# Stores of weight and matrix forms on GpSimd's queue, and earlier places for block 3's rows and block 2's x

## The chip, the core and the metric

The kernel runs on one core of a Trainium2 chip. A core has TensorE (PE; the trace shows its weight loads apart, as PEld), VectorE (DVE), ScalarE (ACT), GpSimd (POOL) and SyncE (SP), each with a queue of instructions that it works off in order, and 16 DMA engines that move data between HBM and the on-chip memory. The metric is the device time of one execution in microseconds, less is better; times of runs are medians.

## The reference

x has 2048 rows of 640. Its layer norm goes through a Fourier mixing (two products with 640x640 matrices, then two with 2048x2048 matrices) and beside it through a dense layer of 1536 with gelu. All is float32.

```python
xn = layernorm(x)                                   # (2048, 640), eps 1e-5
a = einsum("bsd,ed->bse", xn, dft_hid_re)           # wr
b = einsum("bsd,ed->bse", xn, dft_hid_im)           # wi
y = einsum("ts,bse->bte", dft_seq_re, a) - einsum("ts,bse->bte", dft_seq_im, b)
h = gelu_tanh(einsum("bsd,df->bsf", xn, w1) + b1)
out = x + y + einsum("bsf,fd->bsd", h, w2) + b2
```

## The kernel before

Every product is made of three matmuls of 128x128 by 128x512: an operand is split into a high part (an ACT pass, `AF.Copy` to float32r) and a low part (a DVE subtraction), and high x high, high x low and low x high are added up (`product`, `split`, `form_of`). The kernel therefore needs ACT and DVE for every operand that PE takes. Everything is written out by hand in program order: an instruction that waits holds up all behind it on its engine. DMAs are issued by SP, by ACT and, after the change, by GpSimd.

The rows of x are worked on in four blocks of 512. The dense layer comes first. **Block 0 and block 1** run through a loop over `g`, 24 steps: step `g` makes `hidden(g + 2)` (15 matmuls), `gelu(g + 2)`, and `output(g)` (15 matmuls). Beside the 12 steps of block 1, `second_block(i)` prepares what follows, and `prep_w(k)` turns and splits one part of the 640x640 matrices (wr, wi) into seven "forms" w0 to w6, which `put_w` stores to HBM (`wits`) from a staging buffer `wst`. A `prep_w` step is one of three: k = 0 stores two forms, k = 1 two, k = 2 three; six steps lie in block 1's loop, nine come later.

**Blocks 2 and 3** go through the dense layer together, in a scheme that saves products: their turned rows are combined into sums (a11, a12, a22, s1 to s4, oa, ob), likewise pairs of w1 columns (`sums_w1`, `split_w1`, loaded by `load_rq`). For six pairs q, `head(q)`, `mid(q)` and `finish(q)` make the products on eight PSUM banks, some of which are copied one to another by ACT (`copy_bank`, L803). The first of these pairs begins while block 1 ends: `head(0)` stands between `output(22)` and `output(23)`, and `mid(0)` needs bank 3, in which block 1's first output column was added up. `outs(1, ...)` empties those banks: ACT adds the bias (L344), DVE transposes into one of two small buffers (L347), GpSimd adds to `xo` (L349), and SP stores it (`ys`, L876).

The rows of block 3 come by this way: `ln_apply` (L201) normalises them, 16 DMAs (L203) store them to `xs`, `load_z(3)` reads them back in another order (L234), `turn_z2` and `turn_z1` transpose them (L732, L738).

After the pairs, block 2's outputs and then block 3's are added up by `second(2, ...)` and `second(3, ...)`, 24 steps `n`, each beside `beside_second(n)`. There `formed(k)`, four times, builds the forms of a piece of the mixing matrix, and stores them to HBM as `forms_ab` and `forms_c`; the latter from the one staging buffer `xcst`. `load_xr` loads the rows for the builds, `load_xo(2)` the x that `outs(2, ...)` adds to, into a tile that also holds raw w2 (`wz`), which `late_w2` splits. At last come the mixing's long products, a loop without forms of w to store.

Of the kernel before, what the change touches and what calls it, by code (L numbers as in the profile page):

```python
# [10 lines left out]
F32 = mybir.dt.float32  # L11
# [15 lines left out]
def kernel(  # L27
# [57 lines left out]
    def pool(name, side="left", stack=ctx):  # L85
        return stack.enter_context(tc.tile_pool(name=name, bufs=1, side=side, reuse_waits="tile"))
# [288 lines left out]
        )  # L375

    WEARLY = 2
    stores = []

    def put_away():  # L380
        for f in stores:
            f()
        stores.clear()

    def put_w(w, j, main, odd=None, negative=False):

        n = GWIDE[w] * P
        if A["w"]:
            t = A["w"].tile([P, 2, 3 * P], F32R, tag="wst", bufs=2, name=f"wst{w}_{j}")
        else:  # L390
            A["nst"] = A.get("nst", -1) + 1
            t = A["wst"][:, A["nst"] % 5 * 6 * P :][:, : 6 * P].rearrange("p (a b) -> p a b", a=2)
        split(t[:, 0, : 2 * P], t[:, 1, : 2 * P], main)
        if odd is not None and not negative:
            split(t[:, 0, 2 * P :], t[:, 1, 2 * P :], odd)
        elif odd is not None:
            h, l = t[:, 0, 2 * P :], t[:, 1, 2 * P :]
            nc.scalar.activation(h, odd, AF.Copy, scale=-1.0)
            nc.vector.scalar_tensor_tensor(l, odd, -1.0, h.bitcast(F32), op0=ALU.mult, op1=ALU.subtract)
        stores.append(lambda: (nc.scalar if A["w"] else nc.sync).dma_start(wits[w][j], t[:, :, :n].bitcast(F32)))  # L400
        if len(stores) == 2:
            put_away()

    def prep_w(s):

        j, k = divmod(s, 3)
        if j >= ND:
            return
        if k == 0:
            turn_w(0, j)  # L410
            turn_w(1, j)
            if j + 1 < ND and j != WEARLY - 1:
                load_w(0, j + 1)
                load_w(1, j + 1)
        (r1, r2, r4), (i1, i2, i4) = (
            (A["wt", m][:, : 2 * P], A["wt", m][:, 2 * P : 4 * P], A["wt", m][:, 4 * P :]) for m in range(2)
        )

        if k == 0:
            put_w(0, j, r1, r4)  # L420
            put_w(1, j, i1, i4)
            add(r4, r4, i4)
        if k == 1:
            put_w(6, j, i2, i4, True)
            add(i2, i2, r2)
            put_w(2, j, i2, r4)
            add(r2, r1, r2, ALU.subtract)
            add(r1, i2, r1, ALU.subtract)
            add(i1, i1, r1, ALU.subtract)
        if k == 2:  # L430
            put_w(3, j, r1)
            put_w(4, j, i1)
            put_w(5, j, r2)
        put_away()

    def add(dst, a, b, op=ALU.add):
        nc.vector.tensor_tensor(dst, a, b, op=op)
# [286 lines left out]
    def form_of(name, cc, src, dst):  # L724
        FX[name, cc] = dst
        split(dst[:, 0], dst[:, 1], src)
# [180 lines left out]
    def open_w():  # L907
        es_e.close()
        A["es"] = ExitStack()
        A["w"] = pool("wrawp", stack=A["es"])  # L910
        load_w(0, 0)
        load_w(1, 0)

# [14 lines left out]
    def second_block(i):  # L928

        if i == 0:  # L930
            open_w()
            load_z(2)
            ln_stats(12)
            ln_stats(13)
        if i == 1:
            ln_stats(14)
            ln_stats(15)
        if i == 2:
            ln_scale(12, 4)
            for c in range(12, 16):  # L940
                ln_apply(c)
        if i == 3:
            A["zs"] = place("xc01", (P, 30 * P), F32, name="zs")
            turn_z2(two(0), 0)
            turn_z2(two(2), 2)
            turn_z1(ZT[:, 0], 4)
            load_z(3)
        if i == 4:
            form_of("a11", 0, two(0)[:, 0], lane("as", 5))
        if i == 5:  # L950
            open_xf()
        if i == 6:
            form_of("a11", 1, two(0)[:, 1], lane("xc23", 0))
            form_of("oa", 0, ZT[:, 0], lane("xc23", 1))
            form_of("a12", 0, two(2)[:, 0], lane("xc23", 2))
        if i == 7:
            open_tw()
            turn_z2(ZT, 2)
            turn_z2(two(4), 0)
            turn_z1(A["zs"][:, 6 * TB : 7 * TB], 4)  # L960
            load_xo(1)
            sums_w1(0)
        if i == 8:
            split_w1(0)
            load_rq(1)
        if i == 9:
            form_of("a22", 0, ZT[:, 0], lane("r01", 0))
            form_of("a22", 1, ZT[:, 1], lane("r01", 1))
            add(ZT, ZT, two(4))
            form_of("s1", 0, ZT[:, 0], lane("r01", 2))  # L970
            form_of("s1", 1, ZT[:, 1], lane("r01", 3))

    def forms_s2():
        add(two(4), two(0), two(4), ALU.subtract)
        add(ZT, ZT, two(0), ALU.subtract)
        form_of("s2", 0, ZT[:, 0], A["xfx"][:, 0])
        form_of("s2", 1, ZT[:, 1], XTT[:, 0])

    def forms_s3():
        form_of("a12", 1, two(2)[:, 1], A["xfx"][:, 1])  # L980
        form_of("s3", 0, two(4)[:, 0], XTT[:, 1])
        form_of("s3", 1, two(4)[:, 1], XTT[:, 2])

    def forms_s4():
        form_of("s4", 0, two(2)[:, 0], XTT[:, 3])
        form_of("s4", 1, two(2)[:, 1], XTT[:, 4])

    w_early = {1: (0,), 2: (1,), 3: (2,), 4: (3,), 5: (4,), 6: (5,)}
    gelu(0, acc0)
    gelu(1, acc1)  # L990
    for g in range(NG):
        t, i = divmod(g, NF)
        if t == 0:
            prep_w1(i + 3)
            prep_w2(i + 1)
            load_w1(i + 6)
            load_w2(i + 4)
            first_block(i)
            if i == NF - 1:
                acc = hidden(g + 2)  # L1000
                output(g)

                def fill(k):
                    for e in ((0,), (1, 2))[k]:
                        add_block(xo[0], e, oacc[0][e], f"ot0_{e}", bias=b2c[:, e : e + 1])

                gelu(g + 2, acc, fill)
                outs(0, (3, 4))
            elif i == NF - 2:
                output(g)  # L1010
                gelu(g + 2, hidden(g + 2))
            else:
                acc = hidden(g + 2)
                if i == NF - 3:
                    for j in range(ND):
                        prep_xt(1, j)
                        if j + 2 < ND:
                            transpose_z(1, j + 2)
                gelu(g + 2, acc)
                output(g)  # L1020
        elif i < NF - 2:
            acc = hidden(g + 2)
            gelu(g + 2, acc)
            output(g)
            second_block(i)
            for k in w_early.get(i, ()):
                prep_w(k)
        elif i == NF - 2:
            output(g)
            forms_s2()  # L1030
            head(0)
            forms_s3()
        else:
            output(g)
# [29 lines left out]
    oacc[2] = [bank(k) for k in (0, 1, 2, 3, 4)]  # L1064
    oacc[3] = [bank(k) for k in (5, 6, 7, 3, 4)]

    sums_w1(1)
    split_w1(1)
    load_rq(2)
    form_of("ob", 0, A["zs"][:, 6 * TB : 7 * TB], HS[:, 0])  # L1070
    outs(1, (0,), yt=lambda n: AB[:, 0], done=False)

    def rest():
        outs(1, (2, 1, 3, 4), yt=lambda n: AB[:, (n + 1) % 2])
        add(two(2), two(2), ZT, ALU.subtract)

    mid(0, rest)
    forms_s4()
# [5 lines left out]
    for q in range(1, NF // 2):  # L1084
        p = q - 1
        if not p % 2:
            act(p, 0, 0)
        sums_w1(q + 1)
        act(p, 0, 1)

        def between():
            split_w1(q + 1)
            load_rq(q + 2)
            act(p, 1, 0)
            act(p, 1, 1)

        mid(q, between)
        if q < NF // 2 - 1:
            head(q + 1)
        else:  # L1100
            split_h(0)
            second(2, 0, 0, HU[0, 0])
            split_h(1)
            for u in (2, 3):
                split_w2(u)
                raw_w2(u + 4, u - 2)
        for k in late_steps.get(q, ()):
            prep_w(k)
        finish(q)
        if q == 4:  # L1110
            prep_w(14)
            for u in range(2, 6):
                raw_w2(u, u - 2)
# [13 lines left out]

    def formed(k):
        build(k)
        nc.sync.dma_start(forms_ab[k], A["xab", k].bitcast(F32))  # L1130
        nc.sync.dma_start(forms_c[k], A["xc", k].bitcast(F32))

    def late_w2(u):
        split_w2(u)
# [3 lines left out]
    def beside_second(n):  # L1138
# [2 lines left out]
            split_h((n + 3) // 2)  # L1141
        for u in {1: (4, 5), 2: (6,), 3: (7,), 4: (8,), 5: (9,), 6: (10,)}.get(n, ()):
            late_w2(u)
        if n in (2, 4, 6, 8):
            formed(n // 2 - 1)
            load_xr((2, 3, 4, 6)[n // 2 - 1])
        if n == 8:
            load_xo(2)
        if n == 9:
            build(4, "ab")  # L1150
        if n == 11:
# [564 lines left out]
```

## Time and profile before

| | |
|---|---|
| median of 2 runs | 877.41 us (877.28 to 877.55) |
| the profiled execution | 876.81 us, its span 875.0 us |
| granted TensorE clock, mean | 0.99 |
| PE busy | 849.2 us (97%) |
| DVE busy | 659.7 us (75%) |
| ACT busy | 354.0 us (40%) |
| POOL busy | 21.2 us (2%) |
| HBM read, written | 114.76 MB, 42.99 MB |

The span runs from the first to the last instruction of the profiled execution. Busy times do not count waiting, nor the issue of DMAs. Time stamps in the rows are microseconds from the span's start. A row of the waits reads: who waited, for whom, microseconds in total, how many times, the longest. A row of a source line ends in first and last start and the shape; the three numbers behind its count are the least, median and greatest duration in ns.

### The profile page before, as it was taken

To read this page: it belongs to the slowest core of one execution; us is meant where nothing else is said; L and a number is where in the kernel's file an instruction comes from. 1 tells how busy PE (TensorE), PEld (TensorE's weight loads), DVE (VectorE), ACT (ScalarE), POOL (GpSimd) and SP (SyncE) were. 2 spreads that over 40 slices of the span, in tenths; PEclk is the share of its full clock that TensorE was granted. 3 is DMA by queue.
4 is the path that set the end of the run, shared out by engine and by line. 5 is a ranking of instruction groups with operands and counts; after the bars stand their busy time and mean duration, and the time that the engine had idled before them with its cause. 6 is when DMAs were issued, how large, how long until landed. Compare 5 with 4: busy or idle time off the path is not lost.

```text
span 875.0 us, 10292 instructions
## 1 busy us (share of the span) xinstructions
PE 849.2 (97%) x3711; PEld 698.5 (80%) x3711; DVE 659.7 (75%) x831; ACT 354.0 (40%) x495; POOL 21.2 (2%) x22
## 2 busy tenths in 40 slices
PE   8999999979999979999999999999999999999997
PEld 6888888757878858788888888888888888888885
DVE  7555746576676847788988798798977998886686
ACT  7352634445565634443433334332322423223241
POOL 0000300020000020000000000000000000000000
PEclk9999999989999989999999999999999999999999
DMA  6756796828658976958693459856575779904364
GB/s 181 221 145 176 180 200 193 206 69 184 203 208 288 385 151 144 190 134 191 154 225 86 86 149 324 229 107 163 134 184 176 240 202 226 325 18 175 121 170 101
DMA packets 213379, 158.45 MB, mean 181 GB/s; under 512 B 82896, under 2 KB 186576, under 8 KB 212816
## 3 DMA queue, kind: packets, MB, share of 16 engines
q1 hardware_dynamic: 205264, 152.16, 65.2%
q10 hardware_dynamic: 8064, 5.64, 2.0%
q8 instruction: 29, 0.48, 0.2%
q14 instruction: 22, 0.18, 0.1%
HBM read 114.76 MB, written 42.99 MB: 180 GB/s over the span
## 4 chain that ended last, share of the span: by engine, by line
PE 74%; DMA 7%; DVE 7%; ACT 4%; SPq 3%; issue 2%; POOL 1%; ACTq 0%; DVEq 0%; POOLq 0%
PE banks L278 23%; PE banks L279 23%; PE banks L277 23%; PE banks L301 4%; DMA forms_c<-xcst 2%; DMA wit<-wst 2%; POOL xo L349 1%; DMA x<-in_A_x_dram 1%; DMA xo<-in_A_x_dram 1%; DMA xs<-x 1%; SPq L876 1%; SPq L364 1%; DMA wraw<-in_A_dft_hid_im_dram 1%; SPq L203 1%; DVE xtt L161 0%
## 5 line engine op out<-in xcount | busy, mean ns | idle before, releaser
L278 PE MATMUL banks<-as,xab 128*128 128x512 f32 x411 | 160.3, 390 | 0.8 <-DVE as L161 0.8
L277 PE MATMUL banks<-as,xab 128*128 128x512 f32 x411 | 160.2, 390 | 0.0
L279 PE MATMUL banks<-as,xab 128*128 128x512 f32 x411 | 160.1, 390 | 0.0
L160 ACT ACTIVATE as<-r 128x1024 fp32r<-128x1024 f32 x80 | 85.0, 1062 | 175.6 <-PE banks L279 148.4
L161 DVE TENSOR_TENSOR as<-r,as 128x1024 fp32r<-128x1024 f32 x80 | 97.2, 1216 | 37.5 <-ACT as L160 37.3
L278 PEld LDWEIGHTS banks<-as,xab 128*128 128x128 f32 x411 | 77.3, 188 | 17.3 <-DVE as L161 1.2
L277 PEld LDWEIGHTS banks<-as,xab 128*128 128x128 f32 x411 | 77.3, 188 | 16.2
L279 PEld LDWEIGHTS banks<-as,xab 128*128 128x128 f32 x411 | 77.3, 188 | 15.9
L277 PE MATMUL banks<-as,xc 128*128 128x512 f32 x224 | 87.1, 389 | 0.0
L278 PE MATMUL banks<-as,xc 128*128 128x512 f32 x224 | 87.1, 389 | 0.0
L279 PE MATMUL banks<-as,xc 128*128 128x512 f32 x224 | 87.1, 389 | 0.0
L160 ACT ACTIVATE as<-rt 128x1024 fp32r<-128x1024 f32 x32 | 34.0, 1063 | 69.8 <-PE banks L279 57.9
L301 PE MATMUL banks<-xtt,xab 128*128 128x512 f32 x240 | 56.7, 390 | 0.0
L301 PEld LDWEIGHTS banks<-xtt,xab 128*128 128x128 f32 x240 | 44.9, 188 | 9.5 <-DVE xtt L161 0.2
L277 PEld LDWEIGHTS banks<-as,xc 128*128 128x128 f32 x224 | 42.1, 188 | 8.8
L278 PEld LDWEIGHTS banks<-as,xc 128*128 128x128 f32 x224 | 42.1, 188 | 8.7
L279 PEld LDWEIGHTS banks<-as,xc 128*128 128x128 f32 x224 | 42.1, 188 | 8.7
L320 DVE TENSOR_TENSOR hs<-ab,hs 128x512 fp32r<-128x512 f32 x24 | 17.6, 735 | 40.2 <-ACT hs L318 40.2
L161 DVE TENSOR_TENSOR as<-rt,as 128x1024 fp32r<-128x1024 f32 x32 | 38.8, 1213 | 5.3 <-ACT as L160 5.3
L497 DVE STREAM_TRANSPOSE r<-raw 128x1024 f32<-128x1024 f32 x32 | 39.5, 1240 | 3.0 <-PE banks L279 2.4
L160 ACT ACTIVATE as<-u 128x1024 fp32r<-128x1024 f32 (+1 forms) x24 | 22.1, 919 | 48.2 <-PE banks L279 48.2
L161 DVE TENSOR_TENSOR as<-u,as 128x1024 fp32r<-128x1024 f32 (+1 forms) x24 | 24.9, 1042 | 18.8 <-ACT as L160 18.8
(328 smaller groups left out, 1610.4 us busy)
## 6 DMA issues: line engine op xcount, KB each, us to landing
raw<-in_A_dft_seq_re_dram SPq DMA_DIRECT2D x64, 256.0 KB, 5.0
raw<-in_A_dft_seq_im_dram SPq DMA_DIRECT2D x64, 256.0 KB, 5.3
ws<-wit SPq DMA_DIRECT2D x15, 384.0 KB, 5.0
x<-in_A_x_dram SPq DMA_DIRECT2D x16, 320.0 KB, 4.2
xs<-x SPq DMA_DIRECT2D x64, 80.0 KB, 1.8
xo<-in_A_x_dram SPq DMA_DIRECT2D x16, 320.0 KB, 6.7
xab<-wit SPq DMA_DIRECT2D x13, 384.0 KB, 4.2
wit<-wstp SPq DMA_DIRECT2D x12, 384.0 KB, 2.9
```

The source lines that it names most:

```text
L160: nc.scalar.activation(h, s, AF.Copy)
L161: nc.vector.tensor_tensor(l, s, h.bitcast(F32), op=ALU.subtract)
L203: nc.sync.dma_start(xs[c % NC * NC + k, c // NC * B : (c // NC + 1) * B], xt[c][k * B : (k + 1) * B])
L277: nc.tensor.matmul(acc, wh, mh, start=first, stop=False, skip_group_check=goes_on)
L278: nc.tensor.matmul(acc, wh, ml, start=False, stop=False, skip_group_check=goes_on)
L279: nc.tensor.matmul(acc, wl, mh, start=False, stop=last, skip_group_check=goes_on)
L301: nc.tensor.matmul(acc, W1[i][:, a, j * P : (j + 1) * P], XT[j][:, b], start=n == 0, stop=n == len(steps) - 1)
L320: nc.vector.tensor_tensor(hs[:, 1], a, hs[:, 0].bitcast(F32), op=ALU.subtract)
L349: eng.tensor_tensor(d, d, yt.rearrange("p (n i) -> p n i", i=B), op=ALU.add)
L364: nc.sync.dma_start(t[q * B : (q + 1) * B], v[:, :, s0 : s0 + B])
L497: nc.vector.transpose(held(pieces[g][2], u).rearrange("p c (n i) -> p c n i", i=B), r.rearrange("p n (c i) -> p c n i", i=B))
L876: nc.sync.dma_start(ys[k][t], xo[t][:, :, c0:c1])
```

## The change

The stores of forms w0 to w6 and of `forms_ab` and `forms_c` are issued by GpSimd, each at once; before, the w stores were gathered in twos and issued by ACT in block 1's loop, by SP later, and the matrix stores by SP. The staging buffer in block 1's loop is one tile with a fixed place for each form. The memory for wr and wi is opened, and their first loads issued, at the end of block 0; the six `prep_w` steps begin one iteration sooner. In `second_block`, the opening of the next pools, block 3's turns, its sums and splits, and the loads behind them move ahead by about one iteration; the two subtractions for s2 and s3 move from `forms_s2` to iteration 9; the second pair's w1 sums, its split, `ob` and the subtraction for s4 move ahead of `output(23)`. `split_h(0)` moves from the last pair to the end of pair 4. `load_xo(2)` moves from step 8, behind the last form stores, to step 6, ahead of that step's build.

```diff
     def put_w(w, j, main, odd=None, negative=False):
         n = GWIDE[w] * P
         if A["w"]:
-            t = A["w"].tile([P, 2, 3 * P], F32R, tag="wst", bufs=2, name=f"wst{w}_{j}")
+            lo = {0: 0, 1: 6, 6: 0, 2: 6, 3: 0, 4: 4, 5: 8}[w] * P
+            t = A["wst"][:, lo : lo + 2 * n].rearrange("p (a b) -> p a b", a=2)
...
-        stores.append(lambda: (nc.scalar if A["w"] else nc.sync).dma_start(wits[w][j], t[:, :, :n].bitcast(F32)))
-        if len(stores) == 2:
-            put_away()
+        nc.gpsimd.dma_start(wits[w][j], t[:, :, :n].bitcast(F32))
...
         A["w"] = pool("wrawp", stack=A["es"])
+        A["wst"] = A["w"].tile([P, 12 * P], F32R, name="wst")
...
     def second_block(i):
         if i == 0:
-            open_w()
             load_z(2)
...
         if i == 4:
             form_of("a11", 0, two(0)[:, 0], lane("as", 5))
+            open_xf()
         if i == 5:
-            open_xf()
-        if i == 6:
             form_of("a11", 1, two(0)[:, 1], lane("xc23", 0))
             form_of("oa", 0, ZT[:, 0], lane("xc23", 1))
+        if i == 6:
             form_of("a12", 0, two(2)[:, 0], lane("xc23", 2))
-        if i == 7:
-            open_tw()
             turn_z2(ZT, 2)
             turn_z2(two(4), 0)
             turn_z1(A["zs"][:, 6 * TB : 7 * TB], 4)
             load_xo(1)
+            open_tw()
+        if i == 7:
             sums_w1(0)
-        if i == 8:
             split_w1(0)
             load_rq(1)
-        if i == 9:
             form_of("a22", 0, ZT[:, 0], lane("r01", 0))
+        if i == 8:
             form_of("a22", 1, ZT[:, 1], lane("r01", 1))
             add(ZT, ZT, two(4))
+        if i == 9:
             form_of("s1", 0, ZT[:, 0], lane("r01", 2))
             form_of("s1", 1, ZT[:, 1], lane("r01", 3))
+            add(two(4), two(0), two(4), ALU.subtract)
+            add(ZT, ZT, two(0), ALU.subtract)
     def forms_s2():
-        add(two(4), two(0), two(4), ALU.subtract)
-        add(ZT, ZT, two(0), ALU.subtract)
         form_of("s2", 0, ZT[:, 0], A["xfx"][:, 0])
+        form_of("a12", 1, two(2)[:, 1], A["xfx"][:, 1])
         form_of("s2", 1, ZT[:, 1], XTT[:, 0])
+        sums_w1(1)
     def forms_s3():
-        form_of("a12", 1, two(2)[:, 1], A["xfx"][:, 1])
         form_of("s3", 0, two(4)[:, 0], XTT[:, 1])
         form_of("s3", 1, two(4)[:, 1], XTT[:, 2])
+        add(two(2), two(2), ZT, ALU.subtract)
+        split_w1(1)
+        load_rq(2)
+        form_of("ob", 0, A["zs"][:, 6 * TB : 7 * TB], HS[:, 0])
...
-    w_early = {1: (0,), 2: (1,), 3: (2,), 4: (3,), 5: (4,), 6: (5,)}
+    w_early = {0: (0,), 1: (1,), 2: (2,), 3: (3,), 4: (4,), 5: (5,)}
...
             if i == NF - 1:
+                open_w()
                 acc = hidden(g + 2)
...
-    sums_w1(1)
-    split_w1(1)
-    load_rq(2)
-    form_of("ob", 0, A["zs"][:, 6 * TB : 7 * TB], HS[:, 0])
     outs(1, (0,), yt=lambda n: AB[:, 0], done=False)
     def rest():
         outs(1, (2, 1, 3, 4), yt=lambda n: AB[:, (n + 1) % 2])
-        add(two(2), two(2), ZT, ALU.subtract)
...
-            split_h(0)
             second(2, 0, 0, HU[0, 0])
...
         if q == 4:
+            split_h(0)
             prep_w(14)
...
     def formed(k):
         build(k)
-        nc.sync.dma_start(forms_ab[k], A["xab", k].bitcast(F32))
-        nc.sync.dma_start(forms_c[k], A["xc", k].bitcast(F32))
+        nc.gpsimd.dma_start(forms_ab[k], A["xab", k].bitcast(F32))
+        nc.gpsimd.dma_start(forms_c[k], A["xc", k].bitcast(F32))
...
+        if n == 6:
+            load_xo(2)
         if n in (2, 4, 6, 8):
             formed(n // 2 - 1)
             load_xr((2, 3, 4, 6)[n // 2 - 1])
-        if n == 8:
-            load_xo(2)
```

More of the change, by code (lines that the diff above doesn't have):

```diff
@@ L377 @@
     WEARLY = 2
[L378 to L383, printed above, removed]
     def put_w(w, j, main, odd=None, negative=False):
@@ L433, in prep_w @@
             put_w(5, j, r2)
-        put_away()
     def add(dst, a, b, op=ALU.add):
```

## The prediction

> **What bounds the kernel now.** I read the page's first lines, then the table of stretches around every place where TensorE idles, then the waits of PE, and last the waits of the engines behind them.
>
> ```profile
> span 875.0 us, 10292 instructions
> PE 849.2 (97%) x3711; PEld 698.5 (80%) x3711; DVE 659.7 (75%) x831; ACT 354.0 (40%) x495; POOL 21.2 (2%) x22
> ```
>
> PE is busy 97% of the span. So no change of order can win more than PE's idle time, plus what PE loses where its clock is low. The table of stretches (span of the stretch, PE busy and its count first, granted clock after POOL) sizes both.
>
> ```profile
> 160.00:180.00 20.00, 17.45 (x73) 13.27 (x72) 13.93 (x18) 7.41 (x12) 0.00 (x0) 1.00 0.80 191
> 180.00:200.00 20.00, 14.41 (x51) 10.91 (x50) 14.77 (x22) 10.87 (x19) 7.26 (x5) 0.83 0.36 85
> 254.00:262.00 8.00, 6.21 (x25) 4.29 (x25) 5.30 (x7) 6.24 (x10) 0.00 (x0) 1.00 0.78 262
> 315.00:330.00 15.00, 9.83 (x33) 7.37 (x32) 12.03 (x21) 5.44 (x10) 6.40 (x5) 0.77 0.65 138
> 355.00:368.00 13.00, 12.18 (x54) 9.76 (x53) 10.07 (x14) 6.39 (x11) 0.00 (x0) 1.00 1.03 186
> 368.00:868.00 500.00, 500.00 (x2207) 414.10 (x2206) 422.67 (x388) 173.31 (x176) 0.00 (x0) 1.00 0.63 171
> ```
>
> The last row is the calm rate: 2206 steps in 500 us, 0.2267 us a matmul (a stretch counts one matmul too many, that which reaches in). At that rate the others lost: 20 - 72 x 0.2267 = 3.7 (call it A); 20 - 50 x 0.2267 = 8.7 (B); 8 - 24 x 0.2267 = 2.6 (C); 15 - 32 x 0.2267 = 7.7 (D); 13 - 53 x 0.2267 = 1.0. A to D together are 22.7 us. B and D hold more than idle time: after their long waits the granted clock means 0.83 and 0.77, the others stay at 1.00. The long waits of PE:
>
> ```profile
> PE banks L277 <- ACT banks L803: 5.0, 1, 5.0
> PE banks L277 <- ACT xtt L160: 3.3, 1, 3.3
> PE banks L278 <- DVE hs L320: 1.5, 2, 1.3
> PE banks L277 <- ACT hs L160: 1.0, 1, 1.0
> ```
>
> L803, the bank copy, is B; xtt is D; hs L320, a late low part of the gelu, is A; hs L160, split_h(0), is C. After 368 us PE never waits, so the change can win in A to D or not at all.
>
> **The change part by part.**
>
> A, the w stores and the rows of block 3. Behind A stand ScalarE and SP, both waiting for stores of w forms:
>
> ```profile
> ACT wst L160 <- DMA wit<-wst: 14.3, 3, 6.2
> SPq L203 <- DMA wit<-wst: 12.2, 3, 5.8
> 118.98 2.10 SPq L234 DMA_DIRECT2D z<-xs  x4
> 135.09 2.34 DVE zs L732 x2
> L203 SPq DMA_DIRECT2D xs<-x x16: 302/420/439, 140.9 to 154.1; - x16
> 156.00 2.12 SPq L234 DMA_DIRECT2D z<-xs  x4
> 165.69 1.24 DVE L732 STREAM_TRANSPOSE zt<-z 128x1024 f32<-128x1024 f32 x1
> ```
>
> ACT waits to overwrite a staging buffer; the worst of it is inside one step, where the third form reuses the buffer of the first. SP's 16 row stores do not read the w forms at all, yet they wait for their landing, so the two share completion semaphores. The rows are therefore stored from 140.9 instead of right behind their layer norm, block 3 is loaded at 156.0 and turned at 165.7. The change gives each form of a step its own place (no wait inside a step), and takes 14 stores out of ACT's queue and 21 and 8 out of SP's. It also puts eight loads of wr/wi ahead of three ys stores and z of block 2. Those loads cost about 4 us of SP (8 x 0.5, as z's four take 2.10), and z lands that much later than its 118.98 issue; its first use is 135.09, so some ten microseconds cover it. I expect the row stores 16 x 0.42 = 6.7 us long from about 130 (an estimate: their layer norm stands ahead of the turn at 135.09 in VectorE's line), z of block 3 issued near 140 instead of 156, and everything behind it one iteration (30 matmuls, 6.8 us) early, as the diff places it. ACT then has no late gelu: A gives 3.7.
>
> The price is that of a store issued by POOL. This trace has none. The nearest rows:
>
> ```profile
> L400 ACTq DMA_DIRECT2D wit<-wst x14: 326/354/583, 122.4 to 163.1; - x14
> DMA to landing us min/median/max: 2.3/2.9/6.5
> L339 SPq DMA_DIRECT2D xo<-in_A_x_dram x16: 312/488/1109, 90.2 to 372.3; - x16
> DMA to landing us min/median/max: 3.6/6.7/9.0
> ```
>
> The same stores from ACT land in 2.3 to 6.5 us (the first landing row), the slowest loads of similar size in 9.0 (the second). I bound a POOL store by 2.3 and 9.0 and take about 4, near the median of the same store with a microsecond for the new queue. A step's first split waits for the step before, so it is late by landing plus its own work of some 2 us less the period of 6.8. At 4 that is below nothing. At 9 it is 4.2 a step, five steps, 21 us; the gelu is used two iterations on (13.6 less some 2 for its three passes), so PE would stall 5 x 4.2 - 11.6, about 9.4.
>
> The Trainium skill (SBUF — State Buffer, section "Who interferes with whom") says that GpSimd cannot write DMA descriptors while VectorE is in a two-port mode, gives tensor_tensor as an operation that has none, and the section above it gives 620 ns against 3100 ns for such a starved DMA. By that a store would take 2.5 us more (an estimate from that page) and land at 6.5, still under the period; the matrix stores priced in D would be late by 3 x 3.8 instead of 3 x 1.3, and the sum would be 866 instead of 859. No run here shows it yet.
>
> B, the forms ahead of the last output. PE's 5.0 us wait is bank 3, which must be emptied by VectorE and refilled by L803:
>
> ```profile
> 177.61 1.22 DVE L437 TENSOR_TENSOR zs<-zs 128x1024 f32<-128x1024 f32 x1
> 183.36 1.29 DVE L161 TENSOR_TENSOR xtt<-zs,xtt 128x512 fp32r<-128x512 f32 x2
> 187.29 1.23 DVE L161 TENSOR_TENSOR tw<-rq,tw 128x1024 fp32r<-128x1024 f32 x1 [1.12 <-ACT tw L160]
> 188.43 0.68 DVE L161 TENSOR_TENSOR hs<-zs,hs 128x512 fp32r<-128x512 f32 x1
> 189.03 0.71 DVE L347 STREAM_TRANSPOSE ab<-banks 128x512 f32<-128x512 f32 x1
> 189.84 0.58 ACT L803 ACTIVATE banks<-banks 128x512 f32<-128x512 f32 x1 [1.51 <-DVE ab L347]
> L349 POOL TENSOR_TENSOR xo<-xo,ab x5: 1265/1287/2280, 189.9 to 195.5; 128x512 f32<-128x512 f32 x5
> 196.59 1.28 DVE L437 TENSOR_TENSOR banks<-banks,fifth 128x512 f32<-128x512 f32 x2
> ```
>
> Let zero be the time at which head(0) ends on PE. Then come output(23) and three pairs, 30 matmuls: t3 is due at 6.8. ACT's copy of "fifth" ends at about 0.9 (0.3 of hand-over and a pass of 0.58, as L803's), s3's first high part at 1.5, and behind it VectorE has s3 1.29, the moved subtraction 1.22, tw 1.23, ob 0.68, transposition 0.71, to 6.4 with overlaps; L803 0.58 and a hand-over: t3 starts near 7.05, a stall of 0.25. Next GpSimd's adds of 1.29 pace the two buffers of the transpositions: bank 6 is empty at 10.55, where head(1) wants it at 9.8 (0.8), and the second "fifth" add ends at 13.05, where t4 is due at 12.0 (1.1). About 2.1 remain, none over 1.2; the waits of A, up to 1.3, left the clock at 1.00, so I count no half clock. B gives 8.7 - 2.1 = 6.6.
>
> C, split_h(0) ahead of prep_w(14). Its high part is a 128x1024 pass, its low part 1.23 as tw's. ACT has the hole for it just there:
>
> ```profile
> L160 ACT ACTIVATE as<-r 128x1024 fp32r<-128x1024 f32 x80 | 85.0, 1062 | 175.6 <-PE banks L279 148.4
> 252.34 1.23 ACT L160 ACTIVATE wstp<-wz 128x256 fp32r<-128x256 f32 x3 [1.29 <-DVE wz L437]
> ```
>
> 1.06 in 1.29. Without that hole ACT's bank copy behind it would be a microsecond late. I leave 0.3: C gives 2.3. The 21 w stores leaving SP in 200 to 255 cost and win nothing: PE runs on there.
>
> D, forms of the matrices and x of block 2.
>
> ```profile
> 277.92 5.76 DMA forms_c<-xcst
> 293.32 5.69 DMA forms_c<-xcst
> 301.14 1.23 DVE L161 TENSOR_TENSOR hs<-pb,hs 128x1024 fp32r<-128x1024 f32 x1
> 304.72 0.39 PE L277 MATMUL banks<-hs,xc01w 128*128 128x512 f32 x1
> 305.81 8.99 DMA xo<-in_A_x_dram
> 315.01 3.79 POOL xo L349 x3
> DVE ot L347 <- POOL xo L349: 10.7, 3, 9.7
> ```
>
> SP issues xo behind four pairs of form stores that each wait for VectorE. So xo lands at 314.8, GpSimd cannot free the transposition's buffers, VectorE stands 9.7 us and PE's xtt is late. Two steps earlier and with no store before it, xo can go as soon as its tile is free (about 289, in front of the third build, at one build in 7.7 us), and even 9 us lands it at 298. GpSimd has its stores ahead of the adds, but the last of them is ready near 301, one build behind 293.32, and the adds are wanted after 304.72. All 7.7 go.
>
> What is late next: the chain runs from one xcst store's landing to the next build (277.92 to 293.32 is two of them). A store that is slower by 1.3 (a new queue, and row loads that no longer stand behind it) makes three builds 3.9 late; hs ends at 302.4 for 304.72, a cover of 2.35. I charge 1.6. D gives 6.1. The two ends: nothing, or 9.0 instead of 5.7, 9.9 late, 7.6 charged.
>
> **Sum.** 3.7 + 6.6 + 2.3 + 6.1 = 18.7. The profiled execution took 876.8, its span of 875.0 and 1.8 around it; 876.8 - 18.7 = 858.1. The median of the runs shown, 877.4, is 0.6 above it: 858.7.
>
> **Rivals.**
>
> Late forms. POOL's stores of xcst land in 9.0: A, B, C as above, D wins 7.7 and pays 7.6: 877.4 - 12.6 - 0.1 = 864.7. For it: the stores now share the engines with xo's rows instead of standing ahead of them. Against: the rows show 5.7 every time.
>
> The queue does not matter. The row stores stay behind the w stores for a shared semaphore, or for the engines; then the turns put one iteration sooner merely wait in VectorE's line, and A and B stay. C and D remain: 877.4 - 8.4 = 869.0. Against: SP waits for landings, not for bytes; the engines are 0.36 to 0.80 busy. The Trainium skill (DMA: Bandwidth & Descriptors, section "Issuing engines are not separate DMA queues") speaks for this one: it says that all issuers use the same 16 engines and that another issuer saves only issue time.
>
> Slower. The place is wst: each step's first split waits for the last step's POOL store. The stall is 5 x (landing - 4.8) - 11.6; it eats the whole 18.7 from a landing of 10.9 on. At 12 it is 24.4: 877.4 - 18.7 + 24.4 = 883.1, and over 2% from 14.4 on. Against: no store in this trace takes over 6.5.
>
> **How the numbers follow.** Forecast 0.65 (its own range 853.8, all five losses of 23.7 gone, to 862), late forms 0.16, the queue 0.12, slower 0.07. The range 853.8 to 868 takes the forecast, late forms, and w stores at 9 us (858.7 + 9.4). Two per cent, about what a measurement of this kernel can tell from no change, is 17.5: 859.9. The forecast's own range lies about three quarters below it: faster 0.50; slower over 2% about half of the last rival, 0.04; the rest, 0.46, within.
>
> **What would show it.** Right: SP's row stores no longer wait for w stores, block 3 is loaded near 140, its turn is near 150, xo lands before 300, the clock stays at 1.00 from 160 to 330, and the same stretches lose about 0, 2, 0.3 and 1.6. Wrong: waits of ACT for wst grow, PE still waits several microseconds for L803, xcst's landing is over 8, or new PE waits stand after 368.

## The result and the profile after

The changed kernel takes **865.65 us** (median of 2 runs, 865.6 to 865.7) against 877.41: a ratio of 0.9866, 95% interval 0.9824 to 0.9908. Its profiled execution took 865.7 us, its span 863.9. That is 11.8 us won where 18.7 were forecast: a gain clear of no change, and less than the 2% on which the prediction put 0.50. The page's first lines:

```profile
span 863.9 us, 10322 instructions
PE 845.8 (98%) x3711; PEld 696.9 (81%) x3711; DVE 659.7 (76%) x831; ACT 354.3 (41%) x495; POOL 45.1 (5%) x65
```

The table of stretches (columns as before; A and B lie where they lay, C now at 242 to 250, D at 290 to 305):

```profile
160.00:180.00 20.00, 20.00 (x90) 16.53 (x90) 17.42 (x25) 11.72 (x19) 0.00 (x0) 1.00 0.46 93
180.00:200.00 20.00, 18.84 (x81) 14.65 (x80) 11.32 (x17) 10.27 (x17) 6.30 (x5) 1.00 0.68 144
242.00:250.00 8.00, 7.41 (x34) 5.79 (x33) 5.16 (x8) 5.58 (x10) 2.09 (x3) 1.00 0.75 268
290.00:305.00 15.00, 8.82 (x30) 6.44 (x29) 6.92 (x12) 8.06 (x15) 1.99 (x3) 0.77 0.73 305
```

The first stretch is full now and the clock is 1.00 up to 290. But 290 to 305 looks like 315 to 330 did before: 30 matmuls, clock 0.77. The waits of PE name it (the last columns: total, times, longest):

```profile
PE banks L277 <- ACT hs L160: 5.7, 1, 5.7
...
PE banks L277 <- DVE banks L428: 0.8, 1, 0.8
PE banks L277 <- ACT banks L794: 0.6, 1, 0.6
PE banks L278 <- DVE hs L161: 0.5, 1, 0.5
PE banks L277 <- DVE ab L347: 0.4, 1, 0.4
```

Of the waits for the bank copy (L803, now L794) one of 0.6 is left, and that one lies in C. `xtt` is gone, and in its place stands `hs`, the split of the gelu for step 12 of block 2.

PE's order is the same in all kernels here, 3711 matmuls. So I count by matmul number: the time from one start to another, less 0.2267 us for each matmul between. A is matmuls 670 to 760, B 760 to 890, C 1020 to 1220, D 1220 to 1440 (all worked out from the traces, one profiled execution of each kernel):

| loss, us | A | B | C | D |
|---|---|---|---|---|
| before | 3.7 | 8.8 | 2.6 | 8.0 |
| forecast | 0 | 2.1 | 0.3 | 1.6 |
| after | 0.0 | 2.0 | 0.9 | 8.7 |

A, B and C gave 12.2 us of 12.6. **D gave nothing**: the old loss went and one of the same size came 60 matmuls earlier. How that comes about is in the timelines (start, duration, instruction; in brackets the idle time before it and who ended it). POOL's, of the `forms_c` stores alone:

```profile
266.07 0.54 POOL L1123 DMA_DIRECT2D forms_c<-xcst  x1 [1.28 <-DVE xcst L428]
276.44 0.54 POOL L1123 DMA_DIRECT2D forms_c<-xcst  x1 [4.07 <-DVE xcst L428]
284.38 0.53 POOL L1123 DMA_DIRECT2D forms_c<-xcst  x1 [1.63 <-DVE xcst L428]
298.64 0.53 POOL L1123 DMA_DIRECT2D forms_c<-xcst  x1 [9.43 <-DVE xcst L428]
```

Their landing, from the view of their line, and below it that of the same four stores before:

```profile
DMA to landing us min/median/max: 3.9/6.8/12.0
```

```profile
DMA to landing us min/median/max: 5.6/5.7/5.9
```

SP's timeline beside them, ACT's, and VectorE's:

```profile
279.00 2.81 SPq L339 DMA_DIRECT2D xo<-in_A_x_dram  x4
```

```profile
296.44 1.04 ACT L582 ACTIVATE xcst<-asb 128x256 fp32r<-128x256 f32 x2 [10.22 <-DMA forms_c<-xcst]
```

```profile
298.47 1.23 DVE L161 TENSOR_TENSOR hs<-pb,hs 128x1024 fp32r<-128x1024 f32 x1
```

The stores are 10.4, 7.9 and 14.3 us apart; before, they stood 7.7 us apart (277.92 to 293.32 for two steps). Each build must wait until `xcst` has landed. In order, the landings took 8.1, 5.6, 12.0 and 3.9 us, where every one had taken 5.6 to 5.9. So the three builds were 9.5 us late, for a cover of 2.35 us, and `hs`, which stands behind the last build in ACT's and DVE's line, was late by the rest: PE waits 5.7 us for its high part and 0.5 for its low part. What D loses beyond these waits is clock: the trace grants half of it for 6.8 us from 296.6 on, which is the 0.77 of the stretch. The third store was issued 5.4 us after the first of xo's loads. What the 16 DMA engines did from 280 to 288, by queue (packets, MB, share of 16 engines):

```profile
q1 hardware_dynamic: 2233, 1.60, 99.2%
q0 software_dynamic: 68, 0.40, 13.0%
```

And from 288 to 297:

```profile
q0 software_dynamic: 362, 2.99, 78.8%
q1 hardware_dynamic: 358, 0.81, 22.8%
```

From 280 to 288 SP's queue (q1), xo above all, held the engines; POOL's queue (q0) moved 0.40 MB, and 2.99 MB only from 288 to 297. Most of the 0.40 MB is the end of the store before: by the packets in the trace, POOL's queue moved one packet from 281.5 to 287, though the third `forms_ab` had been issued at 282.21. The first packet of that store came 5.2 us after its issue, where the two before it took 2.4 and 2.0.

### The profile page after: what moved, and what is told of

It reads as the page before. It is cut to its first block, busy times and chain, and to the rows that moved or that the text cites. A ratio compares the mean times of both kernels' runs of the same rounds, so it can differ in the third digit from the quotient of the medians.

```text
span 863.9 us, 10322 instructions
## 1 busy us (share of the span) xinstructions
PE 845.8 (98%) x3711; PEld 696.9 (81%) x3711; DVE 659.7 (76%) x831; ACT 354.3 (41%) x495; POOL 45.1 (5%) x65
## 4 chain that ended last, share of the span: by engine, by line
PE 87%; issue 6%; DVE 2%; DMA 2%; POOL 1%; ACT 1%; SPq 0%; POOLq 0%; ACTq 0%; DVEq 0%
PE banks L278 26%; PE banks L279 26%; PE banks L277 26%; PE banks L301 9%; DMA forms_c<-xcst 1%; POOL wit L394 1%; DMA x<-in_A_x_dram 0%; DVE rt L488 0%; DMA raw<-in_A_dft_seq_re_dram 0%; POOL xo L349 0%; PE banks L664 0%; DVE hs L161 0%; DVE st L185 0%; DVE wz L428 0%; POOL forms_ab L1122 0%
```

## The experiments

Two theories for D. **Shared engines**: xo's loads hold the DMA engines for some 8 us, and what is issued behind them lands late. **Software queue**: a store issued by POOL is slow by itself. Two more questions concern A and B: which of the queue, the places and the order won them. Losses are counted as above, from one execution of each kernel; the times are medians and stand beside runs of the kernel before on the same chip, so ratios are compared. A loss in D also holds what the clock takes after a long wait: half clock for 6.8 us after the change; of the runs below, by their traces, for 3.4 in 1, 4 and 6, twice 3.4 in 2, 6.8 in 3, 10.2 in 9, and not at all in 5, 11 and 12. Differences of a microsecond or two in D can therefore be clock alone.

**1. Form stores back on SP.**

```diff
-        nc.gpsimd.dma_start(forms_ab[k], ...); nc.gpsimd.dma_start(forms_c[k], ...)
+        nc.sync.dma_start(forms_ab[k], ...); nc.sync.dma_start(forms_c[k], ...)
```

> The changed kernel with the stores of forms_ab and forms_c issued by SP again; xo of block 2 stays at n == 6. After the change the third xcst store landed 12.0 us after its issue and PE then waited 5.7 us for hs. Theory 'shared engines': xo's loads (640-byte rows) hold the 16 DMA engines for some 8 us whoever issues the store that comes behind them, so from SP the third xcst store lands in 10 us or more again, PE waits 4 to 7 us for hs, and the time is 863 to 868 us. Rival 'software queue': a store issued by POOL is slow by itself, so from SP all xcst stores land in 5.6 to 6 us as before the change, the wait for hs is under 1 us, and the time is 857 to 859 us.

863.71 us, ratio 0.983 (0.9807 to 0.9853). The stores' line with their landing, and the wait of PE:

```profile
L1123 SPq DMA_DIRECT2D forms_c<-xcst x4: 319/323/345, 266.6 to 296.4; - x4
...
DMA to landing us min/median/max: 4.7/5.9/12.0
```

```profile
PE banks L277 <- ACT hs L160: 2.9, 1, 2.9
```

The third landing is 12.0 us again, from SP: the long landing is not POOL's alone. (From SP the store stands behind xo in the same queue; from POOL it stands in another, and is as late.) The stores are 7.8, 8.0 and 14.0 us apart, so what SP's queue does save is the lateness of the first (2.7 us), where SP keeps the row loads behind the stores. The builds are 6.7 us late in all, and D loses 5.9 instead of 8.7.

**2. xo at n == 8, form stores on POOL.**

```diff
-        if n == 6:
-            load_xo(2)
         if n in (2, 4, 6, 8):
             formed(n // 2 - 1)
             load_xr((2, 3, 4, 6)[n // 2 - 1])
+        if n == 8:
+            load_xo(2)
```

> The changed kernel with the form stores on POOL, and xo of block 2 loaded at n == 8 again, behind the rows of that step. Theory 'shared engines': xo is issued near 290, behind the third pair of form stores; the third xcst store lands in 6 to 8 us, PE's wait for hs falls below 1.5 us, xo still lands by about 303 where GpSimd wants it, and the time is 857 to 860 us. Rival 'software queue': the third xcst store still takes about 12 us, and the time is 865 us or more. A third way: xo lands after 305, VectorE waits for GpSimd's adds, and the gain goes back there: 861 to 866 us.

866.28 us, ratio 0.9854 (0.9836 to 0.9871). The landings of the `forms_c` stores, the wait of PE, and that of POOL between 284 and 320:

```profile
DMA to landing us min/median/max: 5.5/8.2/8.8
```

```profile
PE banks L277 <- ACT hs L160: 1.9, 1, 1.9
```

```profile
POOL xo L349 <- DMA xo<-in_A_x_dram: 9.8, 1, 9.8
```

In order they are 7.8, 5.5, 8.6 and 8.8 (from the trace). With xo behind them no store takes 12 us any more; so xo caused that. But the builds are still 5.6 us late without it, and xo comes late again: 4.5 us are lost at `hs` and 5.2 behind POOL's wait for xo. That is the third way of the expectation, dearer than it said. Neither of the two places tried for xo is good in this chain as it stands. The second store, which was issued 4.3 us behind its `forms_ab` instead of about 2, landed in 5.5 us here and in 5.6 in the changed kernel, as from SP before. So POOL's queue alone does not make a store land in 8 or 12 us.

**3 and 4. The same bytes of xo in other shapes.** Why does xo hold the engines so long? It is four loads, each into 32 partitions, in rows of 640 bytes.

```diff
 # 3: runs of 10,240 bytes into 32 partitions
+  src = x[t * TB + q * P : t * TB + (q + 1) * P].rearrange("(r m) (k d) -> r (m k) d", m=4, d=DQ)
+  nc.sync.dma_start(xo[t][q * B : (q + 1) * B], src)
 # 4: runs of 2,560 bytes into 128 partitions
+  src = x[t * TB + q * P : t * TB + (q + 1) * P].rearrange("p (k d) -> p k d", d=DQ)
+  nc.sync.dma_start(xo[t][:, q * 4 : (q + 1) * 4], src)
```

> The changed kernel; the four loads of xo of block 2 read the same bytes of x, 1.31 MB, as runs of 10,240 bytes instead of 640 (the values of block 2's x then stand in other places: that part of the result is left out). Theory 'packets': the engines are held for 8 us by 2048 small packets, not by the bytes, since they moved some 160 to 250 GB/s then against 370 to 440 GB/s beside it; with long runs xo takes 3 to 4 us of the engines, the third xcst store lands in 6.5 to 9 us instead of 12.0, the loss at 292 to 303 falls from 8.7 to 3 to 5.5 us, and the time is 860 to 863 us. Rival 'bytes': the landing stays at 11 us or more, the loss at 8 us or more, and the time at 865 to 867 us.

> The changed kernel; the four loads of xo of block 2 read the same bytes of x, 1.31 MB, but each writes all 128 partitions (2560 bytes in each) where each wrote 32 partitions before (10,240 bytes in each). The values of block 2's x stand in other places, so that part of the result is left out. Long runs into 32 partitions had moved at the same low rate as the 640-byte rows: an engine moved 13.7 bytes per ns in a packet of 10,240 bytes of xo, 12.5 in one of 640, against 25 to 27 in the rows xr and the form stores, which all cover 128 partitions. Theory 'partitions': a load into 32 partitions at a time runs at half the rate, so these loads hold the engines for some 3.3 us instead of 5.6 to 6.5, the third xcst store lands in 8 to 9.5 us instead of 12.0, the loss at 292 to 303 falls from 8.7 to 4.5 to 6.5 us, and the time is 861.5 to 864.5 us. Rival 'source': reading this tensor is slow whatever it is written to; the landing stays at 11.5 us or more, the loss at 8 us or more, the time at 865 to 867 us.

The first: 866.41 us, ratio 0.9864 (0.9843 to 0.9885), D loses 9.4. The second: 864.98 us, ratio 0.9852 (0.9832 to 0.9872), D loses 6.4. SP's queue from 279 to 288 in the first, and the landings of its `forms_c` stores:

```profile
q1 hardware_dynamic: 333, 1.63, 78.4%
```

```profile
DMA to landing us min/median/max: 3.8/6.8/12.4
```

The same of the second, from 278 to 288:

```profile
q1 hardware_dynamic: 849, 1.93, 61.4%
```

```profile
DMA to landing us min/median/max: 4.1/6.7/10.2
```

"Packets" fell: with a seventh of the packets the queue still moved only 1.63 MB in 0.784 x 9 us of 16 engines, 14.4 bytes per ns of packet time, against 12.6 in the changed kernel (1.60 MB in 0.992 x 8 us). Into 128 partitions it moved 19.6 (1.93 MB in 0.614 x 10 us), and the typical packet of 2560 bytes took 102 ns, 25 bytes per ns. Rows sixteen times as long helped little; 128 partitions with shorter rows than those, from the same tensor, did help. So it is the 32 partitions that halve the rate of a packet. The loss in the profiled execution fell as expected (4.5 to 6.5), the landing less (10.2 for 8 to 9.5), and the time came out 0.5 us above its bounds. That execution was the fastest of its four, by 1.1 us, and by the ratios the time cannot be told from the changed kernel's. So the rate is shown, and a gain in time is not.

**5. A second home for xcst**, so that the fourth build does not wait for the third store.

```diff
+    homes_c[3] = lambda: A["tw"].tile([P, 4, TB], F32R, tag="tw0", bufs=1, name="xcst3") ... [:, : 14 * P]
```

> The changed kernel with one edit: the low-order forms of the fourth matrix (xcst of build 3) go into the place that the first buffer of the twiddles leaves free after split_h(5), so that build 3 no longer waits for the landing of the third xcst store. xo stays at n == 6 and the stores on POOL; the third store may still land after 12 us. Theory 'landing behind xo': that wait was the whole of the new loss at 292 to 303 us (8.7 us after the change); PE no longer waits several microseconds for hs, the loss there is 0 to 1.5 us, and the time is 857 to 860 us. Rival 'saturated engines': the 16 DMA engines are busy 99% in that stretch, so the next thing that reads or waits on a transfer (rows xr, the place of forms_ab) takes the wait over: 4 us or more are still lost there, 862 to 867 us.

859.19 us, ratio 0.9801 (0.9766 to 0.9836); three executions took 858.7 to 859.3, one, which was not profiled, 865.6. The landings, ACT's wait between 284 and 305, and PE's:

```profile
DMA to landing us min/median/max: 5.5/10.1/12.3
```

```profile
ACT xab L582 <- DMA xr<-xs: 4.9, 2, 3.5
```

```profile
PE banks L277 <- DVE ot L347: 1.2, 1, 1.2
```

The store still takes 12.3 us, and nobody waits for it: D loses 1.5 instead of 8.7. This shows the chain. What is left has the rival's form: the rows `xr` for build 4 land late behind xo, and the transpositions of the outputs stand behind that build.

**6. The same with the form stores on SP.**

> As the run with two homes for xcst, and the stores of forms_ab and forms_c issued by SP again. From SP the first xcst store landed in 5.9 us against 8.1 from POOL, since SP keeps the row loads behind the stores. Theory 'landing behind xo': both lateness terms (2.6 us of the first landing, 6.5 us of the third) are gone, the loss at 292 to 303 is under 0.5 us, and the time is 856.5 to 858.5 us, equal to the run with POOL or up to 1.5 us below it. Rival 'saturated engines': 4 us or more still lost there, 862 us or more.

859.71 us, ratio 0.9793 (0.9778 to 0.9807), not to be told from run 5; in its profile, the slowest of its four executions (861.28), D loses 4.1. The expectation was wrong: it had under 0.5 lost and 856.5 to 858.5 us. SP holds the row loads behind the stores, and those rows are what is waited for next, as the waits between 280 and 305 have it:

```profile
ACT xab L582 <- DMA xr<-xs: 8.1, 4, 6.5
PE banks L277 <- DVE ot L347: 2.2, 1, 2.2
```

**7. Only the w stores on POOL**, in the kernel before.

```diff
-        stores.append(lambda: (nc.scalar if A["w"] else nc.sync).dma_start(wits[w][j], ...))
-        if len(stores) == 2:
-            put_away()
+        nc.gpsimd.dma_start(wits[w][j], ...)
```

> The kernel before with one edit: every w store issued by POOL at once behind its split; the two staging buffers and the order stay. Theory 'queue': SP's row stores no longer wait for w stores (12.2 us of waits gone), block 3 is loaded near 145, the late gelu of stretch 160 to 180 (3.7 us) disappears, and the stretch 180 to 200 keeps its 8.7 us, since the order of the forms there is unchanged: 873 to 875 us. Rival 'the queue does nothing alone': ACT still waits for its two staging buffers, now for landings of some 4 us instead of 2.9, and the gelu stays late: 876 to 880 us.

879.17 us, ratio 1.0003 (0.999 to 1.0015). SP's row stores and, in the view of their own line, the loads of z:

```profile
L203 SPq DMA_DIRECT2D xs<-x x16: 372/431/1911, 130.5 to 140.0; - x16
```

```profile
L234 SPq DMA_DIRECT2D z<-xs x12: 315/488/549, 71.2 to 143.7; - x12
```

The rows go out from 130.5 instead of 140.9 and the last load of block 3 is issued at 143.7 instead of 157.4: the queue does what the prediction said. Yet A loses 2.6 (3.7 before), B 8.8, C 3.5 and D 9.0, and the time does not move, as the rival had it. ACT still waits for its two staging places, 19.6 us in 7 waits where it was 14.3 in 3, and the order still asks for the rows at the old place.

**8. Only the order of the forms**, in the kernel before (the edits of `second_block`, `forms_s2` and `forms_s3`, with the pool `tw` and that of wr and wi opened as before).

> The kernel before with only the order of the forms changed: turns of block 3 and the forms of block 1's and 2's matrices one iteration earlier, the last forms and the second twiddle step ahead of block 1's last outputs, as in the change. The w stores stay on ACT's and SP's queues with two staging buffers, so the rows of block 3 come back as late as before (loaded near 156). Theory 'rows first': the turns stand in VectorE's line some 5 to 10 us before their rows are there, the gelu behind them is late, and what the stretch 180 to 200 gains (8.8 to 2.0 us) is lost again at 150 to 180: 874 to 882 us. Rival 'order alone': the order is worth its 6.7 us without the queue: 868 to 872 us.

882.78 us, ratio 1.0052 (1.0037 to 1.0067). The turn of block 3 in VectorE's timeline, and PE's longest wait:

```profile
163.65 1.25 DVE L732 STREAM_TRANSPOSE zt<-z 128x1024 f32<-128x1024 f32 x1 [6.62 <-DMA z<-xs]
```

```profile
PE banks L277 <- ACT hs L318: 9.3, 1, 9.3
```

B falls from 8.8 to 4.1, but A rises from 3.7 to 12.4: the turn waits 6.6 us for its rows, the gelu stands behind it. Alone, the order loses.

**9. w stores on the old queues**, each still issued at once, all else as changed.

```diff
-        nc.gpsimd.dma_start(wits[w][j], ...)
+        (nc.scalar if A["w"] else nc.sync).dma_start(wits[w][j], ...)
```

> The changed kernel with the stores of the w forms on ACT's queue (14 of them) and SP's queue (the late ones) as before the change, each issued behind its own split; everything else as changed. Theory 'queue': the row stores of block 3 share completion semaphores with the w stores again and wait for their landing, block 3 is loaded after 150, and the losses of 160 to 200 come back in good part, because the turns that now stand one iteration earlier wait in VectorE's line: 870 to 877 us. Rival 'places and order': what paid was a place of its own for each form and the earlier order, not the queue: 864 to 868 us.

867.01 us, ratio 0.9857 (0.9838 to 0.9876). A loses nothing in its stretch and 1.4 ahead of it, at matmul 630 (147 us); B loses 2.3, C 0.3, D 9.5. Its row stores and the landing of all its w stores:

```profile
L203 SPq DMA_DIRECT2D xs<-x x16: 370/424/1301, 136.8 to 145.2; - x16
```

```profile
DMA to landing us min/median/max: 2.3/2.9/6.7
```

The rows leave at 136.8 even so, and no row store waits for a w store's landing. By these traces POOL's queue is worth 1.7 us ahead of A and in B, and costs 0.6 in C; the times show no difference from the changed kernel.

**10. Two staging places instead of one for each form**, all else as changed.

```diff
-            lo = {0: 0, 1: 6, 6: 0, 2: 6, 3: 0, 4: 4, 5: 8}[w] * P
+            A["nw"] = A.get("nw", -1) + 1
+            lo = A["nw"] % 2 * 6 * P
```

> The changed kernel with the forms of wr and wi staged in two places in turn, as before the change, instead of a place for each form of a step; stores on POOL and the order as changed. Theory 'places': ACT waits for landings inside a step again (before: 14.3 us in 3 waits), the late gelu of 160 to 180 comes back with 2 to 4 us, and the time is 867 to 871 us. Rival 'places do not matter': steps begin an iteration earlier, so the late form is not waited for: 864 to 867 us.

870.3 us, ratio 0.9917 (0.9896 to 0.9938). A loses 3.9, B, C and D as after the change to within 0.3. ACT's wait between 120 and 182:

```profile
ACT wst L160 <- DMA wit<-wst: 19.3, 9, 4.3
```

With the new order, the place for each form is what keeps the gelu in time; it is worth more than the queue.

**11 and 12. A better version**: two homes for xcst, `build(4, "ab")` behind `outs(2, ...)`, and then also the late w stores from SP.

```diff
 # 11, on top of 5
-        if n == 9:
-            build(4, "ab")
         if n == 11:
             outs(2, (3, 4, 0, 1, 2))
+            build(4, "ab")
 # 12, on top of 11
+        (nc.gpsimd if A["w"] else nc.sync).dma_start(wits[w][j], ...)
```

> Two homes for xcst as in that run (stores on POOL), and build(4, 'ab') moved from n == 9 to behind outs of block 2 at n == 11. With two homes 1.5 us were still lost at 297, where VectorE waited for rows of build 4 that landed some 10 us after their issue, behind xo, and the transpositions of the outputs stood behind it. Theory 'next in line is the row load': the outputs no longer stand behind it, the loss at 292 to 303 is under 0.4 us, and the time is 857 to 858.5 us, about 1.5 us below the run with two homes. Rival: build 4 is then late itself for its use from n == 16 on, or its 9 passes push the next split of the gelu, and 1 us or more comes back at 303 to 320.

> As the run with build(4, 'ab') behind outs of block 2, and the 21 late w stores (wstp) issued by SP again; the 14 early ones stay on POOL. With all w stores on the old queues the loss near 245 us (stretch C) was 0.26 us, with POOL 0.8 to 0.9. Theory 'the late stores land later from POOL': C falls to about 0.3, and the time is 856.5 to 858 us, 0.6 us below the run before it. Rival 'chance of order': C stays at 0.8 and the time does not change, or SP, now waiting for the late forms, delays the loads of w2 and of rows and 0.5 us or more is lost elsewhere.

857.37 us, ratio 0.9758 (0.9734 to 0.9782), and 856.7 us, ratio 0.9758 (0.9735 to 0.978). Both beat the kernel before by 2.4% and the changed one by 1.1%. D loses nothing in either, and C 0.8 and then 0.5; between the two no difference in time can be told. The last one's stretch 290 to 305 (its span is 855.2 us):

```profile
290.00:305.00 15.00, 15.00 (x68) 12.43 (x67) 12.79 (x21) 8.03 (x16) 6.67 (x6) 1.00 1.05 362
```

67 steps in 15 us, as many as the calm rate gives, with the DMA engines full. B's 2.0, C's 0.5 and the 1.1 that lay at 355 to 368 before are left.

## Why the prediction was right or wrong

The time lies in the stated range, but outside the forecast's own (853.8 to 862): it is near the rival "late forms" (864.7, given a chance of 0.16), not near the forecast of 858.7, and the mechanism in D is that rival's. The range holds the time because it was made to take that rival in. Of the signs of being wrong that it named, an xcst landing over 8 came; and the clock did not stay at 1.00 up to 330. Step by step:

**A** (3.7 forecast, 3.7 won). Right in sum; the details were later than said, as the row stores' line and VectorE's timeline show:

```profile
L203 SPq DMA_DIRECT2D xs<-x x16: 367/428/1258, 133.2 to 141.7; - x16
```

```profile
156.77 1.24 DVE L723 STREAM_TRANSPOSE zt<-z 128x1024 f32<-128x1024 f32 x1
```

The rows leave from 133, not 130, and the turn is at 156.8, not near 150; it waits for nobody there. SP does not wait for w stores. ACT's waits for its staging did not go, as the view of 120 to 182 has it:

```profile
ACT wst L160 <- DMA wit<-wst: 14.2, 6, 3.7
```

It was 14.3 in 3 waits, the longest 6.2; now they are shorter and no gelu is late for them. Runs 7, 8 and 10 sharpen the reason: it needs the places and the order with the rows; neither the queue nor the order alone wins. The rival "the queue does not matter" is refuted in what it said would follow: A and B did not stay. In the old order the queue does free the row stores (130.5 against 140.9 in run 7). But with the new places and order the old queues do nearly as well (run 9, rows from 136.8), so in its name the rival was close to right.

**The price of a POOL store** (about 4 us taken for the w forms). The landing row is for all 35 w stores of the changed kernel, the 14 of block 1's loop and 21 later ones:

```profile
L394 POOL DMA_DIRECT2D wit<-wst x14: 542/542/705, 117.3 to 155.2; - x14
...
DMA to landing us min/median/max: 2.4/4.1/7.1
```

Taken apart by the trace, the 14 that the prediction priced landed in 4.2 (median, 2.9 to 7.1), against 4.0 from ACT in the same order (run 9), and the 21 later ones in 3.8, against 2.7 from SP. So the 4 was right, but the early stores owe only 0.2 of it to POOL's queue, and the late ones about 1. The rival "slower" needed 10.9.

The Trainium skill (SBUF — State Buffer, section "A bandwidth-pool intuition that's wrong (but worth ruling out)") gives 620 ns against 3100 for a DMA issued by GpSimd beside a VectorE copy; from it came my estimate of 2.5 us more and a sum of 866. That the time is 865.65 is luck for this sum. The runs do not bear out the reading: the stores cost 0.2 to 1 us more, and the loss in D came from SP as well (run 1). Nor did it have to hold here: the Trainium skill (SBUF — State Buffer, section "Who interferes with whom") says that tensor_tensor has no two-port mode. Beside the stores from 262 to 300 VectorE ran tensor_tensor and a few scalar_tensor_tensor, and no copy. The other rule of the Trainium skill, that all issuers use the same 16 engines and interleave there (DMA: Bandwidth & Descriptors, section "Issuing engines are not separate DMA queues"), agrees with run 1 as to the shared engines: 12.0 us from either issuer. Interleaving is not what the changed kernel's trace shows from 281.5 to 287, where POOL's queue moved one packet.

**B** (2.1 to remain, 2.0 remain). Right, and in its parts: 0.2, 0.7 and 1.1 us are lost one behind the other (by matmul number), forecast as 0.25, 0.8 and 1.1. The two rows of PE's waits that belong to it, 0.4 for the transposition at L347 and 0.8 for the add at L428, are the second and the third.

**C** (0.3 to remain, 0.9 remain). The mechanism is the one named, ACT's bank copy late behind the split: the wait of 0.6 for L794. The term was too small by 0.6, which run 9 (0.3) and run 12 (0.5) put on the late w stores from POOL.

**D** (1.6 to remain, 8.7 remain) is the step that failed. Xo landed in time (288.5) and the 9.7 us wait of VectorE was gone, as said. Wrong was the price of moving it: I counted its landing (9 us, hidden) and not the engine time that its four DMAs take ahead of the store on which the builds hang. The xcst landing was taken as 7.0 three times, 3.9 us late in all; it was 8.1, 5.6 and 12.0, and the builds came 9.5 us late. My dear end held that lateness (9.9), but not the loss: 7.6 were charged there and 8.7 came, since I had put nothing for the clock, and half clock followed the wait of 5.7. I saw the collision, in the rival's "for", and let "5.7 every time" outweigh it, though those rows came from an order in which no xo stood ahead.

The lateness has two causes that do not add up: xo ahead of SP's stores makes the builds 6.7 us late (run 1), POOL's stores without xo ahead 5.6 (run 2), both together 9.5. So the stores on POOL were underpriced even without xo (3.9 taken). I put that down to the row loads, which SP no longer keeps behind the stores; it fits the first store of run 1 (5.8 from SP, 8.1 from POOL), but no run kept the rows behind POOL's stores, so it is argued and not shown. That the wait for the third landing made most of the loss is shown by run 5, which took away only the fourth build's wait: D falls to 1.5.

The Trainium skill states the rest (SBUF — State Buffer, section "Door 1: The DMA port swizzle"): a transfer's rate goes by the SBUF ports that its partitions reach, and 32 partitions reach 8 of 16. The trace agrees: 12.6 and 14.4 bytes per ns of packet time into 32 partitions (the changed kernel and run 3), 19.6 into 128, and 25 in the typical packet (run 4). I had not looked it up for xo; by it xo's engine time is twice that of a load of the same bytes into 128 partitions, which is an estimate from that section.

What stays open: why POOL's queue moved next to nothing while xo ran, whether by order of arrival, because its transfers were not yet prepared, or by the way in which the engines choose between queues. The moved `split_h(0)`, the places and the move of xo were not run alone in the kernel before.

## What to carry to other kernels

A load that is moved earlier pays twice: for its landing, which may be hidden, and for the engine time that it takes from whatever is issued behind it. Before moving one, find the transfer whose landing paces the next chain, and either give that chain a second buffer or keep the load behind it. And edits that are nothing or a loss alone (w stores on POOL: 0; order alone: 4.4 us slower) can be worth 10 us together with a third (the places), so cost them as a set.

## What the hardware showed that was not expected

Packets into 32 partitions ran at about half the rate of packets into 128, with rows of 640 and of 10,240 bytes alike. Loads beside them were slowed too: a packet of 2560 bytes of `xr` took 191 ns (median of the 114 from 280 to 288) at the end of xo, and 102 ns (median) from 288 to 297. The store beside the start of xo was not: its packets of 7,168 bytes took 272 ns at both times. And a store's landing under full engines is not a constant of the store: the same 896 KB took 3.8 to 13.1 us over these runs.
